# Threshold attention and a GELU block on one core: the order of work in the first slots

## The chip, the cores and the metric

The kernel runs on one core of a Trainium2 chip. The metric is the device time in microseconds of one execution of the whole program. Before the change it was 1388.04 us, the median of three runs (1387.53 to 1388.61).

## What is computed

All inputs are float32 in meaning; the two weight matrices arrive as float64 and have to be rounded to float32 on the chip.

```python
# q, k, v: (8, 8, 576, 64)     tau = 0.02
scores = (q @ k^T) / 8
keep   = scores >= max(scores) - tau
attn   = softmax(where(keep, scores, -1e9))
x      = (attn @ v), heads put side by side     # (4608, 512)
out    = gelu_exact(x @ w_in) @ w_out           # w_in (512, 2048), w_out (2048, 512)
```

## The kernel before

**Two heads at a time.** The 64 heads are taken as 32 pairs. A pair's 576 queries are cut into chunks of 128 and a tail of 64, so a pair has five *slots* `(p, i)`: chunk `i` of pair `p`, where `i = 4` (`NC`) is the tail of both heads in one. The main loop (from line 828 or so, variable `n`) walks over the slots. The first 20 slots (`n < BATCH`) belong to pairs 0 to 3, called early: first chunks 0 and 1 of the four pairs, `n` = 0 to 7, then chunks 2, 3 and 4 of the four pairs, `n` = 8 to 19.

**One slot.** `scores` multiplies on TensorE (L353) into a PSUM tile `sc`, of which there are two buffers, one for each head. `softmax_head` takes the negated maxima on VectorE (L365), the threshold on GpSimd (L366) and the exponential on ScalarE (L368). `softmax_tail` applies the mask and sums on VectorE (L384), which frees `sc`. For early pairs GpSimd then adds to the sum (L387); `diagonal` takes its reciprocal on VectorE (L395) and puts it on a diagonal on ScalarE (L398). One slot later `turn_p_early` multiplies the probabilities by that diagonal on TensorE (L295), which turns and divides them at once, and ScalarE copies the result into `pT`. `weigh_v` multiplies by v (L470) into `x_blk`.

**Turning q and k.** `turn_qk_early(p)` turns an early pair's q and k by products with an identity (L266, L276), and ScalarE copies them to `qT` (L269, with `q_scale`) and `kT` (L271, L278, L279). For pair 0 this is done ahead of the loop, for pairs 1 to 3 at the end of slot `(p, 0)` of the pair before. `q_scale` and `tau_eff` are made from `tau` by four small operations on VectorE (L787 to L791).

**Rounding the weights.** The weights come in 32 pieces of 128x512 float64, each loaded twice, once shifted by three bytes (`load_piece`, L146 and L148). `conversions` rounds a piece with four operations on VectorE (L168, L174, L176, L178) and one on ScalarE (L169). It is a generator that yields after each step with a price in ns; `convert(ns)` adds `ns` to a debt and takes steps until the debt is paid. The loop calls it once in a slot, after the mask. At most four pieces are on their way or waiting: the last step of one piece (L178) asks for another.

**The MLP.** `fill` puts products of the GELU block (L545, L559) between the slots by a plan `GOAL` over `n`. When all slots are done, a last part runs on TensorE (L679, `strassen`). The rest of the order is written out by hand: each engine works off its instructions in the order in which the program emits them.

**Loads.** q, k and v of the early pairs are loaded by `load_early` and `load_v_early`, those of later pairs by `load`. Small pools decide the buffers: `ld` has two buffers for each of q and k, `xg` has seven of 4 KB a partition, for pieces and for `x_blk`.

Of the kernel before, what the change touches and what calls it, by code (L numbers as in the profile page):

```python
# [8 lines left out]
FP32 = mybir.dt.float32  # L9
# [9 lines left out]
def kernel(  # L19
# [28 lines left out]
    nc = tc.nc  # L48
    ctx.enter_context(tc.manual_schedule())

    B, H, S, D = q.shape
    d_model, d_ff = moe_w_in.shape
    P = 128
    Q = 32
    HP = H // 2
    NP = B * HP
    EARLY = HP
    NC = S // P
    MAIN = NC * P
    TAIL = S - MAIN  # L60
# [4 lines left out]
    N_DF = d_ff // P  # L65
# [23 lines left out]

    warm = const.tile([P, 2], FP32, name="warm")  # L90
    nc.vector.memset(warm, 0.0)
    ident = const.tile([P, P], FP32, name="ident")
    make_identity(nc, ident)

# [19 lines left out]

    w_in_sb = [const.tile([P, d_ff], FP32, name=f"w_in{c}") for c in range(N_DM)]
    w_out_sb = [const.tile([P, d_model], FP32, name=f"w_out{j}") for j in range(N_DF)]


    PIECE = 512
# [63 lines left out]

    conv = {"steps": None, "debt": 0.0}

    def convert(ns):

        if conv["steps"] is None:
            conv["steps"] = conversions()
        conv["debt"] += ns  # L190
        while conv["debt"] > 0:
            took = next(conv["steps"], None)
            if took is None:
                return
            conv["debt"] -= took


    st = {}
# [2 lines left out]
    def load(p):  # L201
        for _ in load_steps(p):
            pass
# [23 lines left out]
    def load_early(p):  # L227
        b, hp = divmod(p, HP)
        s = st[p] = {}
        for name, src in (("q", q), ("k", k)):  # L230
            t = s[name] = ld.tile([P, 2, NC + 1, D], FP32, tag=name, name=name)
            eng = (nc.scalar, nc.gpsimd)[p] if p < 2 and name == "k" else nc.sync
            for e in range(2):
                rows = src[b, 2 * hp + e, 0:MAIN, :]
                if name == "q":
                    eng.dma_start(t[:, e, 0:NC, :].rearrange("p (g c) d -> p g (c d)", c=2),
                                  rows.rearrange("(g p c) d -> p g (c d)", p=P, c=2))
                else:
                    eng.dma_start(t[:, e, 0:NC, :], rows.rearrange("(p t) d -> p t d", p=P))
            eng.dma_start(t[0:TAIL, :, NC, :], src[b, 2 * hp:2 * hp + 2, MAIN:S, :].rearrange("e s d -> s e d"))  # L240

    def load_v_early(p):
        b, hp = divmod(p, HP)
        t = st[p]["v"] = v_sb[p % 4]
        for e in range(2):
            nc.sync.dma_start(t[:, e, 0:NC, :], v[b, 2 * hp + e, 0:MAIN, :].rearrange("(p t) d -> p t d", p=P))
            nc.sync.dma_start(t[e * TAIL:(e + 1) * TAIL, e, NC, :], v[b, 2 * hp + e, MAIN:S, :])

    def turn_qk_early(p):


        s = st[p]
        if 2 <= p < HP:
            qT = op.tile([P, MAIN], FP32, tag="o_sb", name="qT")
            kT = pd_tail[p - 2].rearrange("p b i -> p (b i)")
        else:
            qT = ld.tile([P, MAIN], FP32, tag="qT", name="qT")
            kT = ld.tile([P, TAIL + S], FP32, tag="kT", name="kT")
        s["qT"], s["kT"] = qT, kT
        qt = s["q_tail"] = q_tail[p % 4]  # L260
        for name in "qk":
            t = s[name]
            tr = ps.tile([P, NC, P], FP32, tag="mm", name="tr")
            for c in range(NC):
                for e in range(2):
                    nc.tensor.matmul(tr[e * D:(e + 1) * D, c, :], lhsT=t[:, e, c, :], rhs=ident, start=True, stop=True)  # L266
            src = tr.rearrange("p c s -> p (c s)")
            if name == "q":
                nc.scalar.activation(qT, src, AF.Copy, bias=0.0, scale=q_scale)  # L269
            else:  # L270
                nc.scalar.copy(kT[:, TAIL:S], src)  # L271
        tr = ps.tile([P, NC, P], FP32, tag="mm", name="tr")
        for j, name in enumerate("qk"):
            t = s.pop(name)
            for e in range(2):
                nc.tensor.matmul(tr[e * D:(e + 1) * D, j, 0:TAIL], lhsT=t[0:TAIL, e, NC, :],  # L276
                                 rhs=ident[0:TAIL, 0:TAIL], start=True, stop=True)
        nc.scalar.copy(kT[:, S:S + TAIL], tr[:, 1, 0:TAIL])  # L278
        nc.scalar.copy(kT[D:P, 0:TAIL], tr[D:P, 1, 0:TAIL])  # L279
        for e in range(2):  # L280
            rows = slice(e * D, (e + 1) * D)
            nc.scalar.activation(
                qt[rows, e * TAIL:(e + 1) * TAIL], tr[rows, 0, 0:TAIL], AF.Copy, bias=0.0, scale=q_scale[rows])
# [497 lines left out]
                store(n1, m, lo[m], HD)  # L781

    load_early(0)
    tau_sb = const.tile([P, 1], FP32, name="tau_sb")
    nc.sync.dma_start(tau_sb, tau[0].partition_broadcast(P))
    some = const.tile([P, 1], FP32, name="some")
    nc.vector.tensor_scalar(some, tau_sb, 0.0, None, op0=ALU.is_ge)  # L787
    nc.vector.tensor_scalar(q_scale, some, SCALE, None, op0=ALU.mult)
# [2 lines left out]
    nc.vector.tensor_scalar(tau_eff, tau_sb, lift, None, op0=ALU.max)  # L791
    nc.scalar.activation(warm[:, 1:2], warm[:, 0:1], AF.Exp)
    load_early(1)
    for t in q_tail + v_sb:
        nc.gpsimd.memset(t, 0.0)
    for _ in range(2):
        load_piece(nc.sync)
    turn_qk_early(0)
    load_v_early(0)
    load_early(2)  # L800
    load_v_early(1)

    parts = [(range(2), HP), (range(2, SLOTS), HP)] + [(range(SLOTS), 1)] * (NP - HP)
# [28 lines left out]
    for n in range(len(slots) + WEIGH + 1):  # L832
        p, i = slots[n] if n < len(slots) else divmod(n, SLOTS)
        early = p < EARLY
        last = slots[n - 1] if 0 < n <= len(slots) else None
        if p < NP:
            scores(p, i)
            softmax_head(p, i)
        elif n == len(slots):
            ext = weights_in()  # L840
        gelus(0)
        if n == BATCH:
            gelus_held()
        table()
        for args in due:
            weigh_v(*args)
        due = []
        if p > EARLY and i == WEIGH:
            for lo, hi in (0, WIDE), (WIDE, S):
                weigh_v(p - 1, lo, hi)  # L850
            if p == NP:
                divide(p - 1)
        owed += (goal(n) - goal(n - 1)) * BLK_NS * (PARTS[i] if not early and p < NP else 1.0)
        if early:
            fill(owed, tokens)
            owed = 0.0
            table()
        if last and last[0] < EARLY and last[1] < NC:
            turn_p_early(*last)
        if p < NP:  # L860
            softmax_tail(p, i)
        if p < NP and not early:
            turn_p(p, i)
        if p < NP and not early:
            if i == 2:
                regroup(p, 1)
            if i > 2:
                regroup(p, i)
            if i == NC:
                divisors(p)  # L870
        if last and last[0] < EARLY and last[1] == NC:
            turn_p_early(*last)
        if p < HP - 1 and i == 0:
            turn_qk_early(p + 1)
            if p == 0:
                load_early(3)
                load_v_early(2)
                load_v_early(3)
            if p < 2:
                load_piece()  # L880
        if p < HP and i == NC and 0 < p < HP - 1:
            load(p + 3)
        if n == BATCH:
            for t in pd_tail + [turned_p[:, e, h, :, :] for e in range(2) for h in range(2)]:
                nc.gpsimd.memset(t[:, NB:4 * KR, :], 0.0)
        if EARLY < p < NP and i == DIVIDE:
            divide(p - 1)
        if p >= HP and i == 1 and p + 2 < NP:
            loads = load_steps(p + 2)
        if p >= HP:  # L890
            next(loads, None)
        if p >= HP and i == 1 and p + 1 < NP or p == HP - 1 and i == 2:
            scale_q(p + 1)
        if p >= HP - 1 and i == 2 and p + 1 < NP:
            turn_qk(p + 1)
        convert(0 if n == 0 else 2000 if n < 3 else 3800 if n < BATCH - 1 else 1e9)
        if early:
            diagonal(p, i)
        if not early:
            lag[0] = 2 if p < NP else 0  # L900
            fill(owed, tokens)
            owed = 0.0
        if last and last[0] < EARLY:
            if last[1] == 1:
                due.append((last[0], 0, TOK))
            if last[1] == NC:
                due.append((last[0], TOK, S))
        if n == START - 1:
            tokens = TOK
        elif n == BATCH + 1:  # L910
            tokens = S
        elif p > EARLY and i == DIVIDE and p % HP == 0 or p == NP and i == WEIGH:
            tokens = p // HP * S
            leaving += [n for n in AWAY if n in x_blk and (n + 1) * TOK <= tokens]
        elif leaving and i < 2:
            put_away(leaving.pop(0))
# [34 lines left out]
```

## Time and profile before

| engine | busy us | share of the span |
|---|---|---|
| TensorE, products (PE) | 1361.0 | 98% |
| TensorE, weight loads (PEld) | 968.8 | 70% |
| VectorE (DVE) | 892.8 | 64% |
| ScalarE (ACT) | 640.1 | 46% |
| GpSimd (POOL) | 434.4 | 31% |

The span of the profiled execution is 1387.9 us. These shares are averages over very different stages. The early slots end near 150 us; the slots of the later pairs end before 900 us; the rest is TensorE alone, with VectorE busy 30 to 40% of the time. So a busy share of 64% on VectorE says little about the first stage, and a stage has to be read by itself: with the answers on stretches of the span, on waits, and with the timeline, in which each line has a start, a length, an engine, a line of the program, `out<-in`, a count, and in brackets the idle time ahead of it with what ended it.

| stretch, us | PE busy | DVE busy | ACT busy | granted clock | GB/s |
|---|---|---|---|---|---|
| 0 to 10 | 6.17 | 0.76 | 3.80 | 1.00 | 199 |
| 10 to 20 | 9.46 | 7.17 | 7.66 | 1.00 | 296 |
| 20 to 30 | 8.18 | 6.99 | 6.67 | 0.83 | 295 |
| 30 to 40 | 8.11 | 8.94 | 8.30 | 1.00 | 314 |
| 100 to 110 | 9.69 | 9.04 | 7.06 | 1.00 | 265 |

A wait that names a releaser was ended by it, by the record of semaphores; where a wait is for several things, the last to come is named. A matrix product shows as two records in this trace, since each float32 product is carried out in two.

### The profile page before, as it was taken

Reading aid. Unit: us, or ns where it says so; the run is one execution under the profiler, and the core shown is the slowest. Engines: PE = TensorE matmul, PEld = TensorE weight load, DVE = VectorE, ACT = ScalarE, POOL = GpSimd, SP = SyncE. Lnnn points to the kernel's source line nnn. Section 1 sums busy time; section 2 is a strip of 40 time slices with the busy share of each in tenths; the row PEclk is TensorE's granted clock in tenths of the full one; section 3 lists DMA queues with packets and bytes.
Section 4 is the critical chain, followed back from the end, with each engine's and each line's share of the span. In section 5 each row is a group of like instructions: output and inputs, shape, how many; then the busy total and the mean of one; then the engine's idle time right before and its main releaser. Section 6 shows DMA issues by size and latency. Waiting matters only on the chain.

```text
span 1387.9 us, 20217 instructions
## 1 busy us (share of the span) xinstructions
PE 1361.0 (98%) x6728; PEld 968.8 (70%) x6728; DVE 892.8 (64%) x1738; ACT 640.1 (46%) x1161; POOL 434.4 (31%) x895
## 2 busy tenths in 40 slices
PE   8898999999999999999999999999999999999999
PEld 6676557467466466466476475588888888888887
DVE  5988777788888888888888888764142232241330
ACT  6766627447457458348367356241141240330420
POOL 4453254455555555554554551100000000000000
PEclk9999999999999999999999999999999999999999
DMA  8988266567777788787788776500000001001000
GB/s 274 279 296 275 56 150 160 130 160 175 161 168 182 156 189 179 157 197 176 157 199 177 162 181 129 116 0 8 23 1 23 23 1 46 16 0 53 8 9 23
DMA packets 215206, 169.19 MB, mean 122 GB/s; under 512 B 114288, under 2 KB 199600, under 8 KB 215104
## 3 DMA queue, kind: packets, MB, share of 16 engines
q1 hardware_dynamic: 191184, 112.84, 36.3%
q0 software_dynamic: 23488, 54.77, 12.9%
q8 instruction: 55, 0.90, 0.3%
q14 instruction: 47, 0.39, 0.1%
q10 hardware_dynamic: 432, 0.30, 0.1%
HBM read 72.73 MB, written 12.52 MB: 61 GB/s over the span
## 4 chain that ended last, share of the span: by engine, by line
PE 91%; DVE 5%; ACT 2%; issue 1%; DMA 1%; POOL 0%; DVEq 0%; ACTq 0%; POOLq 0%
PE bank L679 35%; PE o_ps L559 16%; PE hT L545 15%; PE sc L353 12%; PE xT L470 10%; DVE p L384 1%; DVE power L176 1%; PE tr L295 1%; ACT p L368 1%; PE tr L266 1%; DMA raw<-in_moe_w_out_dram 1%; ACT diag L398 1%; DVE power L168 1%; DVE w_out L178 1%; DVE w_in L178 1%
## 5 line engine op out<-in xcount | busy, mean ns | idle before, releaser
L368 ACT ACTIVATE p<-sc,nmx 128x576 f32<-128x576 f32 x288 | 201.9, 738 | 267.6 <-DVE nmx L365 267.4
L384 DVE SCALAR_TENSOR_TENSOR p<-sc,thr,p 128x576 f32<-128x576 f32 x288 | 225.3, 816 | 68.8 <-ACT p L368 67.3
L365 DVE TENSOR_REDUCE nmx<-sc 128x1 f32<-128x576 f32 x288 | 205.4, 750 | 65.8 <-PE sc L353 64.9
L545 PE MATMUL hT<-x,w_in 128*128 128x256 f32 x1024 | 241.1, 385 | 0.0
L559 PE MATMUL o_ps<-w_out,g 128*128 128x512 f32 x512 | 236.7, 603 | 0.0
L545 PEld LDWEIGHTS hT<-x,w_in 128*128 128x128 f32 x1024 | 189.5, 190 | 49.2 <-issue 23.5
L366 POOL TENSOR_SCALAR thr<-nmx,tau_eff 128x1 f32<-128x1 f32 x288 | 85.2, 296 | 393.3 <-DVE nmx L365 392.5
L559 PEld LDWEIGHTS o_ps<-w_out,g 128*128 128x128 f32 x512 | 93.0, 189 | 110.2 <-issue 108.6
L470 PE MATMUL xT<-pT,v 128*64 128x256 f32 (+1 forms) x1280 | 163.9, 409 | 0.4 <-issue 0.4
L353 PE MATMUL sc<-kT,qT 64*128 64x288 f32 x960 | 157.0, 431 | 2.0 <-DVE p L384 1.9
L431 DVE STREAM_TRANSPOSE turned_p<-p 128x1152 f32<-128x1152 f32 x112 | 154.4, 1379 | 3.9
L353 PEld LDWEIGHTS sc<-kT,qT 64*128 64x128 f32 x960 | 89.5, 187 | 75.0 <-issue 63.8
L470 PEld LDWEIGHTS xT<-pT,v 128*64 128x64 f32 x1280 | 89.0, 137 | 72.8 <-issue 14.0
L679 PE MATMUL bank<-x,w_in 128*128 128x256 f32 x480 | 116.7, 379 | 0.0
L679 PE MATMUL bank<-w_out,unit 128*128 128x256 f32 x520 | 115.5, 379 | 0.0
L223 POOL DMA_DIRECT2D v<-in_v_dram x208 | 111.2, 538 | 4.4 <-issue 2.4
L679 PEld LDWEIGHTS bank<-w_out,unit 128*128 128x128 f32 x520 | 98.8, 190 | 13.4
L679 PEld LDWEIGHTS bank<-x,w_in 128*128 128x128 f32 x480 | 91.2, 190 | 12.8 <-issue 0.5
L679 PE MATMUL bank<-v,unit 128*128 128x256 f32 x320 | 82.1, 379 | 0.0
L214 POOL DMA_DIRECT2D q<-in_q_dram x104 | 70.9, 687 | 9.8 <-issue 8.9
L679 PE MATMUL bank<-unit,turned_p 128*128 128x256 f32 x320 | 73.1, 379 | 0.0
L531 ACT ACT_TABLE_LOAD x56 | 71.8, 1283 | 1.0
(156 smaller groups left out, 1492.9 us busy)
## 6 DMA issues: line engine op xcount, KB each, us to landing
pT<-turned_p SPq DMA_DIRECT2D x448, 160.0 KB, 3.6
pT<-pd_tail SPq DMA_DIRECT2D x112, 80.0 KB, 3.1
q<-in_q_dram POOLq DMA_DIRECT2D x104, 72.0 KB, 3.3
k<-in_k_dram POOLq DMA_DIRECT2D x104, 72.0 KB, 3.2
inv<-turned SPq DMA_DIRECT2D x56, 128.0 KB, 3.9
v<-in_v_dram POOLq DMA_DIRECT2D x156, 40.0 KB, 3.2
x<-x SPq DMA_DIRECT2D x10, 512.0 KB, 4.8
raw<-in_moe_w_out_dram POOLq DMA_DIRECT2D x8, 512.0 KB, 4.1
```

Source lines behind the costliest of these rows:

```text
L223: eng.dma_start(t[r:P:4, e, 0:n, :], rows[:, r * KR:r * KR + n, :])
L353: nc.tensor.matmul(sc[e][:, h, 0:HALF], lhsT=lhsT, rhs=s["kT"][rows, at:at + HALF], start=True, stop=True)
L365: nc.vector.tensor_reduce(nmx[:, e:e + 1], sc, axis=AXIS.XY, op=ALU.max, negate=True)
L366: nc.gpsimd.tensor_scalar(thr[:, e:e + 1], nmx[:, e:e + 1], -1.0, tau_eff, op0=ALU.mult, op1=ALU.subtract)
L368: nc.scalar.activation(w[:, e * S:(e + 1) * S].rearrange("p (h s) -> p h s", h=2), sc, AF.Exp, bias=nmx[:, e:e + 1], scale=1.0)
L384: nc.vector.scalar_tensor_tensor(row, sc[e][:, :, 0:HALF], thr[:, e:e + 1], row, op0=ALU.is_ge, op1=ALU.mult, accum_out=den[e])
L431: nc.vector.transpose(turned_p[:, :, i // 2, 0:NB, i % 2 * Q:(i % 2 + 1) * Q], w.rearrange("p (e b i) -> p e b i", e=2, i=Q))
L470: nc.tensor.matmul(to, lhsT=s["v"][:, e, c, :], rhs=rhs, start=(c == 0), stop=(c == KR - 1))
L531: nc.scalar.activation(warm[:, 1:2], warm[:, 0:1], AF.Exp)
L545: nc.tensor.matmul(hT[:, j % 2, :], lhsT=w_in_sb[c][:, j * P:(j + 1) * P], rhs=x_blk[n][:, c, :], start=(c == 0), stop=(c == N_DM - 1))
L559: nc.tensor.matmul(o[:, 0:d_model], lhsT=g[j][:, m * P:(m + 1) * P], rhs=w_out_sb[j], start=(j == 0), stop=(j == N_DF - 1))
L679: nc.tensor.matmul(to, lhsT=l, rhs=r, start=start and k == 0, stop=k == len(pairs) - 1, skip_group_check=not start)
```

## The change

Four things are reordered or added, all in the early slots. The aim is that VectorE, TensorE and ScalarE wait less for one another there.

1. `tau` is loaded first, by GpSimd, and pair 0's `kT` is copied by VectorE beside ScalarE's copy of `qT`.
2. Three products of zeros run on TensorE ahead of pair 0's transposes, to raise its clock. The zeros lie in a part of `w_out_sb` that is not yet in use.
3. Pairs 1, 2 and 3 are turned right behind scores, ahead of the turned probabilities of the slot before: pair 1 behind slot (0, 1), pairs 2 and 3 behind slots (1, 0) and (2, 0). For that pair 2's q and k are loaded before the first weight pieces, into buffers of `xg`, and its k on ScalarE's queue; pair 3's follow; the loads of v of pairs 2 and 3 and of pair 5 come later than before.
4. From slot 3 on at least one rounding step (or 700 ns worth of steps in a slot of tails) stands between the maxima and the mask. The steps are taken from the same generator and counted in the same debt, so that less is left for the call after the mask.

```diff
+    tau_sb = const.tile([P, 1], FP32, name="tau_sb")
+    nc.gpsimd.dma_start(tau_sb, tau[0].partition_broadcast(P))
     ident = const.tile([P, P], FP32, name="ident")
...
+    zeros = w_out_sb[N_DF - 1][:, 0:2 * P]
+    nc.vector.memset(zeros, 0.0)
+    idle = ps.tile([P, 2 * P], FP32, tag="mm", name="idle")
+    for _ in range(3):
+        nc.tensor.matmul(idle, lhsT=zeros[:, 0:P], rhs=zeros, start=True, stop=True)
...
-    def convert(ns):
+    def convert(ns, least=0):
...
-        while conv["debt"] > 0:
+        while conv["debt"] > 0 or least > 0:
...
             conv["debt"] -= took
+            least -= took
...
-            t = s[name] = ld.tile([P, 2, NC + 1, D], FP32, tag=name, name=name)
-            eng = (nc.scalar, nc.gpsimd)[p] if p < 2 and name == "k" else nc.sync
+            pool, tag = (xg, "x") if p == 2 else (ld, name)
+            t = s[name] = pool.tile([P, 2, NC + 1, D], FP32, tag=tag, name=name)
+            eng = (nc.scalar, nc.gpsimd, nc.scalar)[p] if p < 3 and name == "k" else nc.sync
...
+        copy = nc.scalar.copy if p else nc.vector.tensor_copy
...
-                nc.scalar.copy(kT[:, TAIL:S], src)
+                copy(kT[:, TAIL:S], src)
...
-    tau_sb = const.tile([P, 1], FP32, name="tau_sb")
-    nc.sync.dma_start(tau_sb, tau[0].partition_broadcast(P))
...
     load_early(1)
+    load_early(2)
...
     load_v_early(0)
-    load_early(2)
+    load_early(3)
     load_v_early(1)
...
             softmax_head(p, i)
+            if p < HP - 1 and i == (1 if p == 0 else 0):
+                turn_qk_early(p + 1)
...
+        if early and n > 2:
+            convert(0, 700 if i == NC else 1)
         if p < NP:
             softmax_tail(p, i)
...
-        if p < HP - 1 and i == 0:
-            turn_qk_early(p + 1)
-            if p == 0:
-                load_early(3)
-                load_v_early(2)
-                load_v_early(3)
-            if p < 2:
-                load_piece()
-        if p < HP and i == NC and 0 < p < HP - 1:
-            load(p + 3)
+        if p < 2 and i == 0:
+            load_piece()
+            load_v_early(p + 2)
+        if p == 1 and i == NC:
+            load(HP)
+        if n == BATCH - 2:
+            load(HP + 1)
```

More of the change, by code (lines that the diff above doesn't have):

```diff
@@ L277, in turn_qk_early @@
                                  rhs=ident[0:TAIL, 0:TAIL], start=True, stop=True)
-        nc.scalar.copy(kT[:, S:S + TAIL], tr[:, 1, 0:TAIL])
-        nc.scalar.copy(kT[D:P, 0:TAIL], tr[D:P, 1, 0:TAIL])
+        copy(kT[:, S:S + TAIL], tr[:, 1, 0:TAIL])
+        copy(kT[D:P, 0:TAIL], tr[D:P, 1, 0:TAIL])
         for e in range(2):
```

## The prediction

> **What bounds the kernel now.** I read the page's chain of waits first, then stretches of the span, then VectorE's waits and the timelines of the first 150 us.
>
> ```profile
> PE 91%; DVE 5%; ACT 2%; issue 1%; DMA 1%; POOL 0%; DVEq 0%; ACTq 0%; POOLq 0%
> ```
>
> The chain lies on TensorE (PE) for 91% of the span. So I ask where it does not. Stretches, with the columns start:end, length, busy us of PE, weight load, VectorE (DVE), ScalarE (ACT), GpSimd (POOL), granted clock, DMA share, GB/s:
>
> ```profile
> 23.00:24.00 1.00, 1.00 (x8) 1.00 (x7) 0.99 (x3) 1.00 (x2) 0.17 (x1) 0.56 1.06 356
> 66.00:149.00 83.00, 77.34 (x484) 57.60 (x484) 73.41 (x160) 53.42 (x115) 34.46 (x69) 1.00 0.74 249
> 300.00:400.00 100.00, 100.00 (x487) 59.98 (x486) 85.23 (x154) 58.79 (x90) 55.29 (x112) 1.00 0.74 167
> ```
>
> From about 150 us on PE is full, in an order that the edits leave as it is: comparing the built programs, PE's instructions differ only in three products at the start and in where the transposes of pairs 1 to 3 stand. So **what the first 150 us lose or gain is passed on one for one to the end**. There the chain runs through DVE, which carries both the softmax and the rounding of 32 weight pieces. Its waits in 0 to 140 us (engine, line, whom it waited for: total us, times, longest):
>
> ```profile
> DVE p L384 <- ACT p L368: 7.8, 18, 1.1
> DVE nmx L365 <- PE sc L353: 7.4, 4, 3.6
> DVE some L787 <- DMA tau_sb<-in_tau_dram: 5.8, 1, 5.8
> DVE power L168 <- DMA raw<-in_moe_w_out_dram: 1.6, 2, 1.1
> ```
>
> And its timeline, with PE's scores and the first rounding steps beside it:
>
> ```profile
> 6.80 0.15 DVE L787 TENSOR_SCALAR some<-tau_sb 128x1 f32<-128x1 f32 x1 [5.81 <-DMA tau_sb<-in_tau_dram]
> 7.24 0.69 ACT L269 ACTIVATE qT<-tr,q_scale 128x512 f32<-128x512 f32 x1 [3.27 <-DVE lift L790]
> 8.70 2.77 PE L353 MATMUL sc<-kT,qT 64*128 64x288 f32 x8
> 11.03 1.42 DVE L365 TENSOR_REDUCE nmx<-sc 128x1 f32<-128x576 f32 x2 [3.58 <-PE sc L353]
> ...
> 14.38 1.24 PE L353 MATMUL sc<-kT,qT 64*128 64x288 f32 x8
> ...
> 29.37 1.42 DVE L365 TENSOR_REDUCE nmx<-sc 128x1 f32<-128x576 f32 x2 [2.72 <-PE sc L353]
> 31.60 0.82 DVE L384 SCALAR_TENSOR_TENSOR p<-sc,thr,p 128x576 f32<-128x576 f32 x1 [0.81 <-ACT p L368]
> ```
>
> The reader is to see three losses: nothing useful on DVE before 11.03; 2.72 us of waiting at 29.37, because PE had pair 2's transposes between pair 0's transposed probabilities and pair 1's scores; and a wait for the exponential in every slot (0.2 us in most, 0.8 to 1.1 in some). The first score products took 2.77 us and the next, of the same shape, 1.24 us.
>
> **What the Trainium skill says.** "TensorE: Matmul & The Clock Gate", Part 1: the array starts at half rate, goes to full after a busy window of about 3.4 us, and falls back after an idle one. The trace agrees on the two rates (2.77 against 1.24 us; granted clock 0.50 from 23.1 to 26.5 and from 50.4 to 57.2, which are one and two such windows), but not on how soon: PE began at 3.78 and, by the spacing of its transposes, went fast only near 12.9. The same page, "Architectural detail", says that VectorE and ScalarE take instructions strictly in order; the trace shows nothing to the contrary, and it is why a rounding step ahead of a mask can hold the mask up. "DMA: Bandwidth & Descriptors", "Issuing engines are not separate DMA queues": another issuing engine saves issue time alone. That fits the trace's issue times (0.83 us for tau on SyncE) and says that tau gains by going first, not by going elsewhere. "VectorE: DVE Perf Modes", Mode 2x_2P: that mode can't read PSUM, so the copy of kT runs at one element a cycle; at the page's 0.96 GHz 512 elements are an estimated 0.53 us. The nearest row, the maximum over 576 elements at 0.74 us, is the upper end; I take 0.6, as ScalarE's copy took (0.59).
>
> **The change part by part.**
> Tau first: GpSimd issues it at about 0.75, and ident, which stands behind it, comes 0.65 us later (one GpSimd issue), at about 2.0; q lands at 3.75, so that is hidden. With the 4.3 us that tau took from issue to landing, it is there near 5, about 1.8 us earlier than at 6.80. Then qT is copied when q's transposes are done (5.9) instead of at 7.24, and kT on DVE beside it rather than behind it.
> Clock: a memset (under 0.3 us, on an idle DVE) and three products of zeros. An hT product of 256 columns is two records of 225 ns (22 records in 4.95 us), 0.45 us; at half clock 0.9; three are 2.7 us, from about 1.3 to 4.0. They may hold q's transposes by 0.3 us, which is the price. If the clock rises near 6 us, k's 16 records take 1.04 us (as at 13.03) rather than 2.12, so kT is ready at 7.0 + 0.6, and the maxima start 1.27 later (15.65 less 14.38): **8.9 instead of 11.03**. If it stays low until 12.9 as before: 8.03 + 0.6 + 2.33 (11.03 less 8.70) = 10.95, no gain. I take 9.0.
> Pairs turned right behind scores: slot 1's scores can't start before slot 0's masks release their PSUM, 3.12 us after the maxima (14.15 less 11.03), so slot 1's maxima come 3.12 + 1.27 = 4.4 later: 13.4. Slot 2's: PE then has pair 1's transposes (2.2, 39.31 to 41.53), turned probabilities (2.4) and scores (1.2) from 13.3: 19.1; DVE itself would be ready at 18.9. Before: 21.39. Slot 3: scores end 2.2 + 2.4 + 1.2 later, at 24.9, with 5.4 us of DVE work beside them; before 29.37: 4.5 gained. Slot 3's 0.81 and more of exponential waits are filled by rounding, so slot 4 starts about 5.2 earlier than 36.43. Against this: between slot 0's and slot 1's scores PE now idles some 2 us, which may drop the clock for one window and cost 2.2 to 4.6 us of that. I take **4 us** up to slot 4.
> Rounding steps between maxima and masks, from slot 3: no work is added. Slots 4 to 7 (36.43 to 65.15) show waits of 0.21, 0.71, 0.35, 0.36, 0.19 and 0.22 us, 2.0 in all; I take **1.5**, since the wait for ScalarE's relu (0.71) need not go. Behind the held mask are queued the den on GpSimd, the reciprocal, the diagonals on ScalarE and the next scores on PE; the step lasts 0.4 to 0.7 us (up to 1.4 for three in a single-head slot) where the exponential takes 0.75 anyway, and the reciprocal comes at the end of the same DVE work, so none of these comes later.
> Slots 8 to 19, 66 to 149 us: DVE idles 83 - 73.4 = 9.6 us, but PE only 83 - 77.3 = 5.7, and its instructions are not fewer. The smaller caps it: **5.7 at most**; I take two thirds, 3.8.
> Loads: pair 5's q, k and v go out two slots later (slot 18 rather than 16). DVE's waits for landed pieces fall at 118 to 127, behind those loads, 2.05 us; they are part of the 9.6 above. Pair 5 is turned at slot 22, past 155 us, and its loads took about 20 us: hidden. Pair 2's go out before the first weight pieces: 0.59 MB at some 300 GB/s are 2 us of delay for pieces first used at about 16, landed at 11.6 to 16.1 before: hidden, barely.
> Sum: 4 + 1.5 + 3.8 = 9.3, so 1388.0 - 9.3 = **1378.7 us**.
>
> **The rivals.**
> All of it: 5.2 + 2.0 + 5.7 = 12.9 saved, 1375.1. For it: DVE has 16.6 us of idle after 11.03 and no new work. Against it: no two engines interlock perfectly, and PE has 93% of that last stretch.
> Clock lost and PE full: the zeros don't raise it, or the gap after the first scores drops it (1.5 up to slot 4), and PE's full stretch gives back only 2.5 of the rest: 1384.0. For it: the two low-clock windows of the trace follow PE gaps of 1.8 and 2.7 us, no longer than the new one.
> Slower: DMA becomes the bound. In the first 140 us 39.0 MB are moved at a mean 279 GB/s, and a faster DVE asks for 300; a rounding step ahead of a mask that waits for a piece then stops the mask and all behind it. At 1.09 us each (the longest such wait) in 12 slots that is 13.1 lost against 9.3 saved: 1391.8. Against it: the slices reach 390 GB/s, four pieces are in flight, and DVE waits for none before 117.
>
> **How the numbers follow.** Forecast 0.52, all of it 0.22, clock lost 0.18, slower 0.08. Between 1373.5 and 1386 lie all but the worst case and the edges of the others. The bound of 0.2% is 2.8 us: faster below 1385.3. Faster 0.88, same 0.05 (the tail of the third case), slower 0.07.
>
> **What would show it.** Right: the first maxima near 9; no wait near 2.7 us for scores; the exponential waits gone from slot 3 on; PE idle in slots 8 to 19 down to some 2 us; no waits for weight pieces; everything past slot 20 shifted as one. Wrong: first scores still 2.8 us long, a granted clock of 0.5 between 12 and 20 us, masks behind rounding steps that wait for a transfer, or a new idle stretch on PE after 150.

## The result, and the profile after

The changed kernel takes 1384.73 us (median of four, 1384.36 to 1385.68) against 1388.18 for the kernel before in the same series: a ratio of 0.9977, 95% interval 0.9959 to 0.9994. A second series on another occasion gave 0.9981 (0.9972 to 0.9990). It is faster, by some 3 us and not by the 9.3 us that were forecast. The chain of waits of the profiled execution (span 1383.9 us), by engine, from the page:

```profile
PE 95%; DVE 2%; DMA 1%; ACT 1%; issue 0%; ACTq 0%; POOL 0%; DVEq 0%; POOLq 0%
```

VectorE's part of the chain fell from 5% to 2%. Its waits in 0 to 140 us (engine, line, whom it waited for: total us, times, longest); L397, L378 and L798 are the mask, the maxima and the first use of tau, L185 the third rounding step and L178 the relu that it needs:

```profile
DVE power L185 <- ACT power L178: 6.2, 3, 4.2
DVE nmx L378 <- PE sc L366: 4.0, 5, 1.5
DVE some L798 <- DMA tau_sb<-in_tau_dram: 3.7, 1, 3.7
...
DVE p L397 <- ACT p L381: 1.2, 4, 0.4
```

The wait for the exponential went from 7.8 us to 1.2, as meant. But a wait that was 0.7 us before, L185 for ScalarE's relu, is now 6.2, and 4.2 of it come at one place. The timeline of the first slots:

```profile
4.92 0.15 DVE L798 TENSOR_SCALAR some<-tau_sb 128x1 f32<-128x1 f32 x1 [3.67 <-DMA tau_sb<-in_tau_dram]
...
7.66 0.69 ACT L282 ACTIVATE qT<-tr,q_scale 128x512 f32<-128x512 f32 x1 [3.73 <-DMA k<-in_k_dram]
...
8.40 1.24 PE L366 MATMUL sc<-kT,qT 64*128 64x288 f32 x8 [0.96 <-ACT qT L282]
...
9.68 1.42 DVE L378 TENSOR_REDUCE nmx<-sc 128x1 f32<-128x576 f32 x2 [1.51 <-PE sc L366]
...
12.29 2.99 PE L366 MATMUL sc<-kT,qT 64*128 64x288 f32 x8 [2.65 <-DVE p L397]
...
22.25 1.33 ACT L178 ACTIVATE power<-power,rebias 128x512 uint32<-128x512 uint32 x2
...
23.00 0.69 DVE L185 SCALAR_TENSOR_TENSOR power<-raw,power 128x512 uint32<-128x512 uint32 x1 [4.21 <-ACT power L178]
...
24.42 1.40 DVE L378 TENSOR_REDUCE nmx<-sc 128x1 f32<-128x576 f32 x2
```

The reader is to see that slot 0 comes earlier (9.68 against 11.03), with its scores at full speed; that TensorE then idles 2.65 us and does slot 1's scores at half speed; that the relu of slot 1 runs at 22.25 (at 19.22 before), behind the copies of pair 1's transposes and of the turned probabilities in ScalarE's queue; and that slot 2's maxima stand at 24.42, **3 us later than the 21.39 of the kernel before**. Stretches of the same profile, with the columns of the prediction (the granted clock is the third number from the end):

```profile
13.00:19.00 6.00, 6.00 (x43) 4.72 (x44) 4.35 (x10) 2.92 (x6) 3.04 (x7) 0.50 1.03 385
163.00:169.00 6.00, 6.00 (x11) 2.58 (x9) 5.71 (x12) 1.41 (x2) 3.04 (x8) 0.50 0.22 65
```

The clock is at a half from 13 to 19 us (by the trace's record of the clock from 12.4 to 19.3), and again from 163 to 169. From 66 to 142 us, a stretch that lies within slots 8 to 19 in both kernels, first the kernel before and then the changed one:

```profile
66.00:142.00 76.00, 70.86 (x440) 52.41 (x440) 67.60 (x148) 48.85 (x105) 33.58 (x66) 1.00 0.81 272
66.00:142.00 76.00, 73.47 (x467) 56.20 (x468) 69.73 (x154) 51.23 (x110) 36.07 (x66) 0.99 0.82 266
```

TensorE's idle time there went from 5.1 to 2.5 us. When the maxima of some slots start (us), in single profiles:

| kernel | slot 0 | 2 | 4 | 8 | 20 | 22 | 24 | span |
|---|---|---|---|---|---|---|---|---|
| before | 11.03 | 21.39 | 36.43 | 65.15 | 147.83 | 164.91 | 175.72 | 1387.9 |
| changed | 9.68 | 24.42 | 36.53 | 63.45 | 142.72 | 159.22 | 172.60 | 1383.9 |
| changed, again (e11) | 9.20 | 22.63 | 34.73 | 63.14 | 142.61 | 159.11 | 170.80 | 1383.6 |
| relu early (e1) | 9.69 | 22.84 | 35.02 | 62.42 | 141.90 | 158.39 | 170.09 | 1383.8 |
| gap filled (e2) | 10.06 | 21.93 | 34.04 | 61.44 | 140.70 | 157.19 | 168.94 | 1380.5 |
| both (e9) | 10.28 | 20.68 | 33.08 | 61.16 | 140.99 | 157.49 | 168.29 | 1380.0 |
| pair 1 put back (e4) | 9.04 | 18.95 | 31.05 | 57.46 | 136.71 | 153.21 | 164.95 | 1378.0 |
| pair 1 put back, slot 23 filled (e10) | 10.62 | 20.54 | 32.65 | 60.78 | 141.58 | 158.08 | 168.88 | 1379.5 |
| no rounding between (e5) | 9.33 | 22.77 | 35.13 | 64.92 | 145.50 | 162.58 | 174.28 | 1385.7 |
| rounding between alone (e7) | 11.16 | 21.45 | 36.15 | 64.73 | 144.71 | 161.20 | 172.01 | 1383.0 |

Executions of one kernel differ by some us: of the kernel before, one series ran from 1384.4 to 1391.2 us. So small gains are read here from the distance between two slots, and from ratios with their intervals, not from one span. A distance too is that of one execution: e4 and e10 are the same program up to slot 22, and slots 4 to 8 took 26.41 us in one and 28.13 in the other.

### The profile page after: what moved, and what is told of

Read it like the earlier page. It is cut to its first block, busy times and chain, and to the rows that moved or that the text cites. A ratio compares the mean times of both kernels' runs of the same rounds, so it can differ in the third digit from the quotient of the medians.

```text
span 1383.9 us, 20232 instructions
## 1 busy us (share of the span) xinstructions
PE 1362.2 (98%) x6734; PEld 969.7 (70%) x6734; DVE 893.2 (65%) x1742; ACT 638.2 (46%) x1158; POOL 437.5 (32%) x896
## 4 chain that ended last, share of the span: by engine, by line
PE 95%; DVE 2%; DMA 1%; ACT 1%; issue 0%; ACTq 0%; POOL 0%; DVEq 0%; POOLq 0%
PE bank L692 35%; PE o_ps L572 17%; PE hT L558 17%; PE sc L366 13%; PE xT L483 11%; PE tr L308 2%; DMA raw<-in_moe_w_in_dram 1%; DVE nmx L378 0%; DMA k<-in_k_dram 0%; DVE power L185 0%; DVE p L397 0%; DVE w_in L187 0%; ACT p L381 0%; PE tr L279 0%; DVE power L177 0%
## 5 line engine op out<-in xcount | busy, mean ns | idle before, releaser
L397 DVE SCALAR_TENSOR_TENSOR p<-sc,thr,p 128x576 f32<-128x576 f32 x288 | 225.4, 816 | 60.3 <-ACT p L381 58.4
L378 DVE TENSOR_REDUCE nmx<-sc 128x1 f32<-128x576 f32 x288 | 205.5, 750 | 66.0 <-PE sc L366 65.2
L379 POOL TENSOR_SCALAR thr<-nmx,tau_eff 128x1 f32<-128x1 f32 x288 | 89.9, 312 | 394.2 <-DVE nmx L378 393.8
L572 PEld LDWEIGHTS o_ps<-w_out,g 128*128 128x128 f32 x512 | 93.9, 191 | 112.0 <-issue 110.4
```

Of the source, the lines that this page charges most:

```text
L378: nc.vector.tensor_reduce(nmx[:, e:e + 1], sc, axis=AXIS.XY, op=ALU.max, negate=True)
L379: nc.gpsimd.tensor_scalar(thr[:, e:e + 1], nmx[:, e:e + 1], -1.0, tau_eff, op0=ALU.mult, op1=ALU.subtract)
L397: nc.vector.scalar_tensor_tensor(row, sc[e][:, :, 0:HALF], thr[:, e:e + 1], row, op0=ALU.is_ge, op1=ALU.mult, accum_out=den[e])
L572: nc.tensor.matmul(o[:, 0:d_model], lhsT=g[j][:, m * P:(m + 1) * P], rhs=w_out_sb[j], start=(j == 0), stop=(j == N_DF - 1))
```

## The experiments

**What slot 1 lost.** Two theories were open: the relu's place in ScalarE's queue, or TensorE's clock.

e1, one rounding step ahead of pair 1's transposes:

```diff
             softmax_head(p, i)
+            if n == 1:
+                convert(0, 1)
             if p < HP - 1 and i == (1 if p == 0 else 0):
                 turn_qk_early(p + 1)
```

> The changed kernel with one rounding step of slot 1 (L177 with its relu on ScalarE) moved ahead of pair 1's transposes, so that the relu no longer stands behind their copies in ScalarE's queue. Theory Q (the 4.2 us wait of L185 in slot 1 is a matter of place in ScalarE's queue): L185 waits under 0.5 us there, slot 2's maxima are then set by the scores (end at 22.9 with the clock still low) and come at about 23.0 instead of 24.4, and the end moves by the same 1.4 us or less: 1383.3. Theory C (the low clock of 12.4 to 19.3 is the cause and the queue only shows it): slot 2's maxima stay within 0.5 us of 24.4.

```profile
18.49 0.69 DVE L185 SCALAR_TENSOR_TENSOR power<-raw,power 128x512 uint32<-128x512 uint32 x1
...
22.84 1.42 DVE L378 TENSOR_REDUCE nmx<-sc 128x1 f32<-128x576 f32 x2 [2.86 <-PE sc L366]
```

In its timeline L185 waits for nothing, yet the maxima of slot 2 now wait 2.86 us for the scores: another wait has taken part of its place. From slot 0 to slot 2 it takes 13.15 us. The changed kernel took 14.74, and 14.66 in e3's profile, which is the same program up to slot 22; in these three the clock was low for 6.8 us. In e11 (13.43) it was low for 3.4 us only, so that e11 can't be set beside e1. Like with like, the place in the queue is worth 1.5 to 1.6 us at slot 2. At the end nothing of it can be told: ratio 0.9973 (0.9959 to 0.9987), not apart from the changed kernel's.

e2, TensorE's gap behind slot 0's scores filled:

```diff
+    def keep_warm(k):
+        t = ps.tile([P, 2 * P], FP32, tag="mm", name="idle")
+        for _ in range(k):
+            nc.tensor.matmul(t, lhsT=zeros[:, 0:P], rhs=zeros, start=True, stop=True)
...
             softmax_head(p, i)
+            if n == 0:
+                keep_warm(5)
```

> The changed kernel with five more products of zeros in the idle gap of TensorE between slot 0's and slot 1's scores (9.6 to 12.3 us); results unused. Theory C: the granted clock stays at 1.00 through 12 to 19, slot 1's scores take 1.24 rather than 2.99 us, pair 1's transposes 2.2 rather than 3.9, slot 2's scores end near 19, L185 waits about 1.5 us instead of 4.2, slot 2's maxima come near 20.5 instead of 24.4, and the end moves by 3 to 4 us to about 1381, unless a later gap falls differently in the clock's windows (2.4 to 3.3 us either way). Theory Q alone: the relu still waits behind the same copies, gain under 1 us.

```profile
12.68 1.94 PE L366 MATMUL sc<-kT,qT 64*128 64x288 f32 x8 [0.29 <-DVE p L397]
...
20.49 0.72 DVE L185 SCALAR_TENSOR_TENSOR power<-raw,power 128x512 uint32<-128x512 uint32 x1 [2.08 <-ACT power L178]
...
21.93 1.40 DVE L378 TENSOR_REDUCE nmx<-sc 128x1 f32<-128x576 f32 x2
```

The clock stayed up, slot 1's scores took 1.94 us (they wait for the second mask in between), slot 0 to slot 2 took 11.87. Ratio 0.9951 (0.9936 to 0.9966). 2.08 us of the relu's wait are left (1.5 were expected), and slot 2 stands at 21.93, not near 20.5.

e9, both edits together:

> The changed kernel with both repairs of slot 1 and pair 1's transposes left where the change puts them: the relu ahead of those transposes, and five more products of zeros in the gap behind slot 0's scores. If the two causes are separate and are all of it, their gains at slot 2 (1.6 us and 2.5 us, each alone) add up or, since the second also shortens what the relu stands behind, a little less: slot 2's maxima at 20.3 to 20.8, L185 waits under 0.5 us in slot 1, and the end 3 to 4 us below the changed kernel, ratio near 0.995. If moving pair 1's transposes back gained by something else, slot 2's maxima stay above 21.5.

```profile
18.26 0.69 DVE L185 SCALAR_TENSOR_TENSOR power<-raw,power 128x512 uint32<-128x512 uint32 x1
...
20.68 1.42 DVE L378 TENSOR_REDUCE nmx<-sc 128x1 f32<-128x576 f32 x2 [0.93 <-PE sc L366]
```

Slot 0 to slot 2 takes 10.40 us, L185 has no wait in slot 1, and slot 2's maxima stand at 20.68, set by the scores. Ratio 0.9957 (0.9941 to 0.9973): the end doesn't separate it from e2, the slots do. The two causes explain the loss, and they add up: 14.7 us in the changed kernel with the clock low for 6.8 us, 13.15 with the queue mended, 11.9 with the clock mended, 10.4 with both.

e4, pair 1's transposes put back between slot 0's and slot 1's scores, where they fill the gap themselves:

```diff
-            if p < HP - 1 and i == (1 if p == 0 else 0):
+            if 0 < p < HP - 1 and i == 0:
                 turn_qk_early(p + 1)
...
+        if p == 0 and i == 0:
+            turn_qk_early(1)
         if p < 2 and i == 0:
             load_piece()
```

> The changed kernel with pair 1's transposes put back where they stood, between slot 0's and slot 1's scores; pairs 2 and 3 as changed. They fill the gap of TensorE (2.2 of 2.65 us) with work that has to be done anyway, and their copies come ahead of slot 1's exponentials on ScalarE. Theories C and Q both say: clock at 1.00 through 12 to 19, no wait of L185 over 1 us in slot 1, slot 2's maxima at 19 to 20.5 instead of 24.4 and the end 4 to 5 us earlier, near 1380, give or take one fall of the clock later (2.4 to 3.3 us). Rival (the early lead is given back in the stretch where TensorE is 93% busy): less than 2 us at the end although slot 2 comes 4 us earlier.

```profile
8.94 1.09 PE L279 MATMUL tr<-ident,q 128*64 128x128 f32 x16
...
11.65 1.94 PE L366 MATMUL sc<-kT,qT 64*128 64x288 f32 x8 [0.37 <-DVE p L397]
```

```profile
17.54 0.69 DVE L185 SCALAR_TENSOR_TENSOR power<-raw,power 128x512 uint32<-128x512 uint32 x1
...
18.95 1.40 DVE L378 TENSOR_REDUCE nmx<-sc 128x1 f32<-128x576 f32 x2
```

TensorE's timeline has pair 1's transposes at full speed straight behind the scores and only 0.37 us of waiting ahead of slot 1's; VectorE's has no wait for the relu and slot 2 at 18.95, 9.91 us after slot 0. Slot 20 comes 11.1 us earlier than before. In e10's execution of the same slots, slot 0 to slot 2 takes 9.92 us as well, but slot 0 comes at 10.62, and slot 20 only 6.3 us earlier than before; so the 9.9 us are of the program, the 11.1 of one execution. 1380.62 us, ratio **0.9941 (0.9925 to 0.9957)**: by the medians this one edit more than doubles the gain of the change.

**What the rounding steps are worth.** e5 takes them out of the changed kernel, e7 puts them alone into the kernel before.

```diff
-        if early and n > 2:
-            convert(0, 700 if i == NC else 1)
         if p < NP:
             softmax_tail(p, i)
```

> The changed kernel without the rounding steps between maxima and masks (all steps back behind the mask). Theory R (these steps alone carry the lead that the changed kernel builds up between slot 4 and slot 20, 106.2 us against 111.4): slot 4 to slot 20 takes 110 to 111.5 us, DVE's waits for the exponential are back at 6 to 7 us, slot 20 comes near 147 and the end near the time of the kernel before, ratio 0.999 to 1.001. Rival (the lead comes from pair 5's later loads or the turned pairs): slot 4 to slot 20 stays within 1.5 us of 106.2.

> The kernel before with the rounding steps between maxima and masks alone added from slot 3 on. Theory R: the first slots stay as before (slot 4's maxima at 36.4 less the 0.8 us wait of slot 3), slot 4 to slot 20 takes 106 to 107.5 instead of 111.4, slot 20 comes near 142.5, and the end is 4 to 5.5 us earlier, ratio 0.9965, as much as the whole change gives, so that the sum of the other parts is about nothing. Rival: under 2 us.

The waits of e5's VectorE in 0 to 140 us:

```profile
DVE p L397 <- ACT p L381: 6.9, 17, 1.0
```

The wait for the exponential is back. Slot 4 to slot 20 takes 110.4 us in e5, 106.2 in the changed kernel (107.9 in e11), 111.4 in the kernel before, 108.6 in e7, over the 107.5 that were expected at most. e5's ratio is 0.9998 (0.9988 to 1.0008), e7's 0.9967 (0.9957 to 0.9977). So at the end this part alone carries the whole gain of the change, and the other parts as a set came to nothing.

Slot by slot it is less plain. Slots 4 to 8 took 28.72 us before and 28.58 in e7, with the clock low from 50.4 to 57.2 us in both: in these two executions the steps alone gained 0.1 us there. Slots 8 to 20 took 82.68 us before, 79.98 in e7, 80.58 in e5 and 79.27 in the changed kernel (79.2 to 79.8 in six other profiles that have the steps and the later loads, 80.8 to 81.6 in the three where the clock fell between slots 18 and 19). There the steps are worth 2.7 us alone and 1.3 on top of the rest, and e5 gains 2.1 us without them. Its waits for the exponential are all there (5.7 us against 6.1), but those for weight pieces are down from 2.1 us to 0.4, with pair 5's loads later; in e7, where these stand as before, they are 2.7. That the later loads did it is argued from these waits; no run moves them alone.

**The zeros.** e6 leaves out the memset and the three products.

> The changed kernel without the memset and the three products of zeros. Theory Z (the zeros raise the clock some 7 us earlier): the first transposes and the first scores run at half rate, first maxima at 10.9 to 11.2 instead of 9.7, and slot 2's maxima 0.5 to 1.5 us later than 24.4; the end moves by about 1 us, ratio near 0.998. Rival (the clock falls again at 12.4 anyway, so the zeros buy nothing that lasts): slot 2's maxima within 0.5 us of 24.4.

The clock rises for the first time at 19.4 us (5.6 with the zeros), and the first maxima come at 11.20, so the zeros do bring slot 0 forward by 1.5 to 2 us. But slot 0 to slot 2 takes 14.1 us there, within what the changed kernel takes, and the ratio is 0.9980 (0.9971 to 0.9989): at the end nothing of it can be told. Without the zeros slot 0's scores take 2.63 us and slot 1's 2.99, both at half speed; with them slot 0's are fast, but the clock has fallen again by slot 1's, which take 2.99 in the changed kernel too. Slot 2 at 25.31 is later than in both executions of the changed kernel, by 0.9 and 2.7 us.

**Pair 2's k on ScalarE.** e8 is e4 with those loads issued by SyncE:

```diff
-            eng = (nc.scalar, nc.gpsimd, nc.scalar)[p] if p < 3 and name == "k" else nc.sync
+            eng = (nc.scalar, nc.gpsimd)[p] if p < 2 and name == "k" else nc.sync
```

> The changed kernel with pair 1's transposes where they stood before, and with pair 2's k issued by SyncE instead of ScalarE. Theory A (qT of pair 0 waits in ScalarE's queue behind these issues, to 7.03 us where its data are there by about 5.9): qT is copied near 6.0, the first scores start near 7.1 instead of 7.76, first maxima near 8.4 instead of 9.0, and the end gains 0.6 over the run with pair 1's transposes put back (ratio 0.9937). Rival (SyncE's queue is now longer ahead of the first weight pieces, so rounding waits for them in slots 1 and 2): slot 3's maxima no earlier than 24.5, ratio 0.9941 or above.

```profile
5.87 0.69 ACT L282 ACTIVATE qT<-tr,q_scale 128x512 f32<-128x512 f32 x1 [1.93 <-PE tr L279]
...
7.58 1.51 PE L366 MATMUL sc<-kT,qT 64*128 64x288 f32 x8 [0.50 <-DVE kT L284]
```

qT is copied at 5.87 instead of 7.03, as soon as its data are there, but then kT sets the scores: slot 0 comes at 8.82 against 9.04 in e4. That is the earliest of the nine profiles that have the zeros and this issue (9.04 to 10.62). In e10, with the same first slots as e4, the issue held qT until 8.61, and the scores began at 9.35, while kT's last columns for them had been copied by 8.39: an estimated 1 us lost there. In e8 VectorE waits 1.9 us for a weight piece later. Ratio 0.9946 (0.9928 to 0.9964): no gain that can be measured at the end.

**The late fall of the clock.** In the changed kernel's profile slot 22 to slot 24 took 13.38 us, before 10.81. TensorE idles 1.6 us ahead of slot 23's scores in both. TensorE's timeline, the kernel before and then the changed one:

```profile
167.52 1.94 PE L353 MATMUL sc<-kT,qT 64*128 64x288 f32 x8 [1.59 <-DVE p L384]
169.39 4.56 PE L559 MATMUL o_ps<-w_out,g 128*128 128x512 f32 x10
```

```profile
161.82 2.95 PE L366 MATMUL sc<-kT,qT 64*128 64x288 f32 x8 [1.58 <-DVE p L397]
164.71 6.89 PE L572 MATMUL o_ps<-w_out,g 128*128 128x512 f32 x10
```

The same ten records take 4.56 and 6.89 us. e3 puts three products into that gap, e10 does so in e4.

```diff
+            if n == 23:
+                keep_warm(3)
             scores(p, i)
```

> The changed kernel with three products (operands at hand, results unused) ahead of slot 23's scores, where TensorE idles 1.6 us at 160.2 to 161.8. Theory L (the changed kernel loses 3.3 us of its lead there because that gap lies inside one window of the clock, which then runs at half rate from 162.6 to 169.4): the clock stays at 1.00 there, slot 24's maxima come near 169.5 instead of 172.6, and the end moves by 2.4 to 3.3 us to about 1381.8. Rival (the lead is lost to VectorE or to loads that come later, and the clock is no cause): no change beyond 0.7 us.

> Candidate for the fastest: the changed kernel with pair 1's transposes put back, and three products ahead of slot 23's scores in TensorE's 1.6 us gap, so that its clock can't fall there. Theory L: slot 22 to slot 24 takes 10.8 us instead of the 11.7 of the run without them (13.4 in the changed kernel), and the end gains 0.9 us or less over ratio 0.9941: 0.9935. Rival (the products themselves delay the scores): slot 22 to 24 at 11 to 12 us, no gain.

TensorE's timeline in e3:

```profile
162.26 1.46 PE L799 MATMUL idle<-w_out 128*128 128x256 f32 x6
164.01 1.94 PE L366 MATMUL sc<-kT,qT 64*128 64x288 f32 x8 [0.29 <-DVE p L397]
165.88 4.56 PE L572 MATMUL o_ps<-w_out,g 128*128 128x512 f32 x10
```

In e3 the clock stays up there, and slot 22 to slot 24 takes 10.81 us, in e10 10.80. Without the products it took 13.38 in one execution of the changed kernel and 11.69 in the other, 11.74 in e4, and 10.8 in e7 and e9. So the gap's fall is shown to cost up to 2.6 us in an execution, but not in each. The trace's record of the clock tells which. In each of the profiles all changes of the clock lie whole multiples of 3.41 us apart (in the changed kernel's at 12.4, 19.3, 63.6, 67.0, 162.6 and 169.4), as the edges of windows would. Where at least 1.16 us of the 1.6 us gap lay within one such window, the clock fell at its end (eight profiles); where an edge split the gap into parts of at most 1.06 us, it did not (the kernel before, e7 and e9).

At the end e3 has 0.9967 (0.9957 to 0.9977) and e10 0.9937 (0.9920 to 0.9954), neither apart from its kernel without the products. In both of their profiles, and in e6's, the clock fell at another place, between slots 18 and 19 (from 134.7 to 138.1 in e3), which took 9.1 us there and 7.6 in the others; in e3 and e10 the products stand behind that place in the program. e10, at 1380.06 us, is the lowest median that was run, not proven faster than e4.

> The changed kernel once more, on the same chip as the two above, to compare with. Slot 2's maxima near 24.4 and L185's wait near 4 us if these are of the program and not of one execution; the fall of the clock behind slot 22 (13.4 us from slot 22 to slot 24) may come out as 10.8, 11.7 or 13.4, since it hangs on where a gap of 1.6 us lies in the clock's windows. Ratio 0.997 to 0.998.

e11 has L185's wait (3.05 us), a low clock from 12.7 to 16.1 (12.4 to 19.3 in the first profile) and slot 2 at 22.63: the loss in slot 1 belongs to the program; its size, from slot 0 to slot 2, differs by 1.3 us between the two executions, as the stretches of low clock do.

## Why the prediction was wrong, point by point

- **The step that failed: slot 2's maxima at 19.1, and the 4 us taken up to slot 4.** The first 36 us gained nothing in the profiled execution and 1.7 us in e11. The term was built from TensorE's work at full speed, "19.1", with VectorE "ready at 18.9". Both halves were off. The working named the gap between the two scores and the low clock as a risk of 2.2 to 4.6 us, and then charged about 1.2 us for it (5.2 less 4); the gap came in both profiles of the changed kernel and in those of e1, e3 and e5, with the clock low for one window or two, and e2 shows it to be worth 1.6 to 2.9 us by slot 2. And "DVE itself would be ready at 18.9" took slot 1's rounding from the kernel before, where the relu was not behind pair 1's transposes; the edit moved those ahead of it in ScalarE's queue. e2 still shows 2.08 us of that wait, and e9 that another 1.5 us go when it is removed. With the transposes put back (e4), slot 2 came at 18.95 and slot 4 at 31.05, 5.4 us earlier than before (3.8 in e10, whose slot 0 is 1.6 later than e4's): near the 5.2 of the working before the gap was charged.
- **The first maxima: 9.0 taken, 9.68 and 9.20 measured.** The clock and kT on VectorE came as worked out. Tau's landing (4.92 against "near 5") did by luck: its issue began at 1.24, not at 0.75, and it took 3.7 us to land, not 4.3. qT "when q's transposes are done" did not: it started at 7.66, because pair 2's k is issued from ScalarE's queue ahead of it (an issue in two parts, to 7.56). That cost was set at nothing; e8 against e4 shows 1.2 us on qT, of which 0.2 reached the first maxima, kT being next; in e10 it was about 1.
- **Pairs 2 and 3 behind scores: right.** The 2.72 us wait for slot 3's scores is 0.27 us, at 29.95.
- **Rounding between maxima and masks: the mechanism right, the sizes in part by luck.** The waits for the exponential went as forecast (7.8 to 1.2 us). Slots 4 to 8 gained 28.72 less 26.92, 1.8 us (1.5 taken), in the first profile, but 0.3 in e11 and 0.1 in e7: how long the clock was low there weighs more. Slots 8 to 20 gained 3.4 us (3.8 taken), and 3.2 in e11; but e5 has 2.1 of it without these steps, with fewer waits for pieces, a gain that was not in the sum. TensorE's idle time was the cap that was named: 2.5 of 5.1 us remain from 66 to 142 us. L185's wait for the relu, which was allowed to stay in slots 4 to 7, went there (0.7 to 0 in both profiles of the changed kernel), but grew from 0.3 to 2.0 us in slots 8 to 19.
- **"What the first 150 us gain is passed on one for one": not quite.** The lead was 5.1 us at slot 20 and 3.1 at slot 24 in the changed kernel's profile; in e11 5.2 and 4.9, in e4 11.1 and 10.8. A shift of the whole moves the gaps of TensorE against the windows of its clock, as the late fall shows. That was not in the sum.
- **Rivals.** "Slower" fell: no mask waited long behind a rounding step, and pieces were waited for 1.2 us in all, 2.7 in e11. "Clock lost" came closest, 1384.0 against 1384.73. It was right about the gap and the clock, and wrong in its second reason: TensorE's full stretch gave near to what was forecast. That the two times come so close is luck: it took a gain of 1.5 us up to slot 4, where the first profile had none, and the fall behind slot 22 wasn't in it. Two readings among the rivals are a little off: VectorE's idle time from 11.03 to 140 us in the kernel before is 16.1 us, not 16.6 (in "all of it"), and the clock fell at 50.4 us within the gap of 2.7 us, after 1.45 of it.

## What to carry to other kernels

Before moving work behind something else, write down what each engine is left with in the place that it leaves: here pair 1's transposes were the filler of a gap of TensorE, and moving them opened it. And follow the moved work's *results* into the queue of the engine that takes them: a small operation of another chain (the relu) stood behind them, and VectorE waited for it. A reordering in several parts is best put in part by part: one part here brought all of the gain, and one cost 3.5 to 4.8 us from slot 0 to slot 2.

## What was not expected of the hardware

A gap of TensorE well under 3.41 us, the length of the windows in which its clock changed here, was enough to halve the clock: 2.35 to 2.65 us ahead of slot 1's scores, in all five profiles that had this gap at full clock (the changed kernel, e1, e3, e5 and e11), and 1.6 us ahead of slot 23's, where it lay mostly in one window, with one or two windows of low clock (0.9 or 2.6 us lost). Idle time in a window is not all: from 135.8 to 139.2 us the kernel before had 1.79 us of it, and the clock stayed up.

Once low, the clock stayed so for 6.8 us in three of these five profiles and for 3.4 in two, although TensorE was busy nearly throughout by its records, with scores and then with transposes (in the changed kernel with no idle time from 12.4 to 15.8 us, the first of its two windows). What decides between one and two is open.

The products of zeros raised the clock: with them it rose at 4.3 to 6.1 us and k's first transposes took 1.14 us for 15 records. Without them these took 2.12 us in e6 and in the kernel before, and the clock rose at 19.4 and at 12.9 us, although the transposes had begun at 3.9 and 3.8. What share of the array must be busy for how long wasn't tried.
